# Three attention pairs turned by transposing DMAs instead of TensorE, gate weights prepared on VectorE, four more dummies, and a new order of all engines

## The chip, the cores and the metric

The kernel runs on one core of one Trainium2 chip. The metric is the time of one execution on the device in microseconds, as the median of several runs. Shorter is better. Engines are called as in the profile: PE (TensorE), with PEld for its weight loads, DVE (VectorE), ACT (ScalarE), POOL (GpSimd), and SP, whose queue issues nearly all DMAs.

## The reference

Attention in which a query sees only the keys of its own hash bucket, and after it an RWKV channel mix. Four batches, 8 heads, 768 positions, 64 values a head; the mix has width 512 and 1024 inner units.

```python
q_bits = (einsum('bhsd,dk->bhsk', q, proj) > 0)      # 6 bits a row; k the same
mask = q_bucket[:, :, :, None] == k_bucket[:, :, None, :]
scores = where(mask, scale * (q @ k.T), -1e9)
attn_out = softmax(scores) @ v                       # then x: [4, 768, 512]
x_prev = x shifted by one position
xk = mu_k * x + (1 - mu_k) * x_prev                  # xr the same with mu_r
k = relu(xk @ w_k);  v = (k * k) @ w_v;  r = sigmoid(xr @ w_r)
return r * v
```

## The kernel before

**Work.** Two heads make a pair; there are 16 pairs, four to a batch. Each pair n goes through these steps (the name that the order uses in front):

- `ldq`, `ldv`: loads of q, k and v on SP's queue.
- `hi`, `lo` (L391, L394, DVE): q and k split into a high and a low fp16 half in `nh`; `tr` (L398, SP): a transposing DMA that brings `nh` into `a`, with positions along the free dimension. Pairs 2 and 3 have one for q and one for k, later pairs one for both.
- `bits` (L418, PE): the six hash projections; `bx` (L421, DVE): their signs; `row` (L438, POOL): copied into rows of `a`, so that a score of rows in different buckets comes out low enough to vanish.
- `sc` (L536, PE): nine score steps of 1024 columns; `exp` (L540, ACT): their exponentials into `pt`.
- `vsum` (POOL) and, from pair 4 on, `mean` (PE) and `va`, `mc` (DVE): v with its mean taken off.
- `oo` (L558, L563, PE): the product with v in three groups a head; `rc`, `ob` (DVE): division into `ob`.
- the turn of `ob` into `xt` (model dimension on partitions). Pairs in `OT_PE` use six PE transposes (`ot`, L591) and one DVE copy out of PSUM (`xt`, L594); all others use a transposing DMA on SP's queue (`otd`, L597).
- `xs`, `df`, `xk`, `xr` and their helpers (DVE): the shift and the two mixtures.

Pairs 0 and 1 have no `tr`: PE turns q and k itself (`y`, L473, and `t`, L504), with `x` (L481), a matmul with the gate weights `pw`, giving their bits. `pw` (L702) is the projection with its sign turned, laid out for two heads; it needs the load `pj`.

When the four pairs of batch b have their mixtures, the channel mix follows: `kp` (L651, PE) with `relu` (ACT) and `sq` (DVE), `r` (L671, PE) with `tanh` (ACT), `v` (L684, PE), `os` (DVE), `st` (SP, the store). `wl` and `wc` load the mix's weights and cast them on POOL; `muk` and `mur` load the two mixing vectors, and a small nameless DVE operation each (L270) takes one off.

At the start PE runs matmuls with zeros, called dummies here (`warm`, L247). They compute nothing that is used.

**Order.** `Plan.add` numbers all operations in the order of the program text and notes their dependencies. `ORDER` is a fixed list of these numbers: every engine issues its own operations in this order, and waits where a dependency is not met. `BANKS` gives each PSUM user its place: steps `sc` and `bits` take two of the eight banks, other users one; a user waits until the one before it in its bank has been read. So an operation can wait for its inputs, for its bank, or for what stands ahead of it in its own queue.

```python
    NWARM = 20
    OT_PE = (0, 1, 2, 3, 15)
        if n in OT_PE:
            add("PE", 6 * 0.056, ft, r=["idb", ("ob", so, 0), ("ob", so, 1)], w=[(nm,)], take=("sm", nm, 0), name=nm)
            add("DVE", DVE_C(768, 2), fx, r=[(nm,)], w=[("xt", sx)], give=[nm], name=f"xt{n}")
        else:
            add("SP", 1.25, fd_, r=[("ob", so, 0), ("ob", so, 1)], w=[("xt", sx)], svc=0.95, tr=1, name=f"otd{n}")
```

Of the kernel before, what the change touches and what calls it, by code (L numbers as in the profile page):

```python
# [13 lines left out]
ALU = mybir.AluOpType  # L14
# [114 lines left out]
def kernel(  # L129
# [13 lines left out]
    nc = tc.nc  # L143
# [15 lines left out]
    NWARM = 20  # L159
# [4 lines left out]
    MERGED = tuple(range(4, 16))  # L164
    FIRSTS = (0, 1)
    ROW_SP = ()
    OT_PE = (0, 1, 2, 3, 15)
    QS = 4.0
    ESC = (D ** -0.5) / (QS * QS)
    BITW = 4096.0  # L170
# [594 lines left out]
```

## Time and profile before

| What | Value |
|---|---|
| median of 3 runs | 246.25 us (245.77 to 246.52) |
| profiled execution | 244.73 us |
| its span | 243.0 us |
| PE busy | 234.2 us (96%) |
| DVE busy | 187.6 us (77%) |
| ACT busy | 182.6 us (75%) |
| POOL busy | 95.9 us (39%) |
| granted PE clock | 1.00 |
| DMA queue of SP | 72272 packets, 43.40 MB, 70.7% of 16 engines |

Times inside the kernel are counted from the start of the span. Busy time is that of the engine's own instructions; the share of the DMA engines is a mean over sixteen and reaches a little over 1 where all are busy. The profiled execution is a single one and is shorter than the three timed ones.

### The profile page before, as it was taken

To read this page: it belongs to the slowest core of one execution; us is meant where nothing else is said; L and a number is where in the kernel's file an instruction comes from. 1 tells how busy PE (TensorE), PEld (TensorE's weight loads), DVE (VectorE), ACT (ScalarE), POOL (GpSimd) and SP (SyncE) were. 2 spreads that over 40 slices of the span, in tenths; PEclk is the share of its full clock that TensorE was granted. 3 is DMA by queue.
4 is the path that set the end of the run, shared out by engine and by line. 5 is a ranking of instruction groups with operands and counts; after the bars stand their busy time and mean duration, and the time that the engine had idled before them with its cause. 6 is when DMAs were issued, how large, how long until landed. Compare 5 with 4: busy or idle time off the path is not lost.

```text
span 243.0 us, 6250 instructions
## 1 busy us (share of the span) xinstructions
PE 234.2 (96%) x2522; PEld 147.3 (61%) x2522; DVE 187.6 (77%) x388; ACT 182.6 (75%) x242; POOL 95.9 (39%) x150
## 2 busy tenths in 40 slices
PE   8998999999999899999999999999999999999994
PEld 6975676765567446465556665465566765455443
DVE  3489899999899989699999989936745476966142
ACT  3689999999989689698877998777679871165230
POOL 5465797885919673428036230093500000000000
PEclk9999999999999999999999999999999999999999
DMA  6989999999999999999989683464310403041033
GB/s 229 370 243 197 219 259 230 356 204 348 245 217 233 367 281 208 259 272 264 222 195 233 155 162 85 146 114 126 120 46 0 35 3 119 0 173 47 0 131 132
DMA packets 72526, 44.01 MB, mean 181 GB/s; under 512 B 54832, under 2 KB 67504, under 8 KB 72496
## 3 DMA queue, kind: packets, MB, share of 16 engines
q1 hardware_dynamic: 72272, 43.40, 70.7%
q8 instruction: 20, 0.33, 0.6%
q10 hardware_dynamic: 224, 0.20, 0.2%
q14 instruction: 10, 0.08, 0.1%
HBM read 24.12 MB, written 6.29 MB: 125 GB/s over the span
## 4 chain that ended last, share of the span: by engine, by line
PE 55%; DVE 6%; DMA 3%; issue 1%; DVEq 0%
PE ps_all L684 15%; PE ps_all L651 13%; PE ps_all L536 11%; PE ps_all L671 8%; PE ps_all L563 6%; DMA a<-nh 3%; PE ps_all L418 2%; DVE xk L636 1%; DVE tm L633 1%; DVE nh L391 1%; DVE nh L394 1%; DVE df L622 0%; DVE os L691 0%; DVE va L373 0%; DVE bx L421 0%
## 5 line engine op out<-in xcount | busy, mean ns | idle before, releaser
L540 ACT ACTIVATE pt<-ps_all 128x1024 bf16<-128x1024 f32 x144 | 139.1, 1040 | 19.8 <-PE ps_all L536 18.7
L536 PE MATMUL ps_all<-a 128*128 128x256 f16 (+1 forms) x384 | 79.2, 325 | 2.0 <-ACT pt L540 1.1
L438 POOL COPY a<-bx 6x384 f32<-6x384 f32 x56 | 38.9, 696 | 54.5 <-DVE bx L421 42.3
L563 PEld LDWEIGHTS <-pt 128*128 128x128 bf16 x1152 | 43.7, 97 | 11.6 <-issue 2.1
L651 PE MATMUL ps_all<-xk,wk 128*128 128x384 bf16 x256 | 49.6, 326 | 0.3 <-DVE xk L636 0.3
L536 PEld LDWEIGHTS <-a 128*128 128x128 f16 x384 | 33.7, 98 | 24.9 <-issue 3.5
L684 PE MATMUL ps_all<-wv,k 128*128 128x512 bf16 (+2 forms) x208 | 46.7, 363 | 0.0
L563 PE MATMUL ps_all<-va,pt 128*128 128x65 bf16 x1152 | 46.2, 193 | 0.4 <-DVE va L373 0.4
L658 DVE TENSOR_TENSOR k<-kr 128x384 bf16<-128x384 bf16 x64 | 25.8, 424 | 14.1 <-ACT kr L655 13.8
L655 ACT ACTIVATE kr<-ps_all 128x384 bf16<-128x384 f32 x64 | 29.6, 497 | 7.7 <-PE ps_all L651 6.7
L651 PEld LDWEIGHTS <-wk 128*128 128x128 bf16 x256 | 24.0, 98 | 15.5 <-issue 0.3
L674 ACT ACTIVATE rs<-ps_all 128x512 f32<-128x512 f32 x24 | 14.3, 603 | 23.0 <-DVE os L691 11.7
L684 PEld LDWEIGHTS <-k 128*128 128x128 bf16 x208 | 19.6, 98 | 19.1
L691 DVE SCALAR_TENSOR_TENSOR os<-rs,ps_all 128x512 f32<-128x512 f32 (+2 forms) x26 | 16.7, 643 | 14.9 <-PE ps_all L684 10.8
L394 DVE SCALAR_TENSOR_TENSOR nh<-nat,nh 128x1536 f16<-128x1536 f32 (+1 forms) x16 | 25.7, 1607 | 0.2
L671 PE MATMUL ps_all<-wr,xr 128*128 128x512 bf16 x96 | 24.5, 379 | 0.0
L349 POOL TENSOR_TENSOR vt<-vn 128x384 f32<-128x384 f32 x12 | 14.4, 1200 | 10.8 <-DMA vn<-in_v_dram 7.1
L581 DVE TENSOR_TENSOR ob<-ps_all,rc 128x384 bf16<-128x384 f32 x32 | 17.5, 552 | 0.7
L391 DVE TENSOR_SCALAR nh<-nat 128x1536 f16<-128x1536 f32 (+1 forms) x16 | 15.8, 989 | 1.5 <-DMA nat<-in_k_dram 0.9
L671 PEld LDWEIGHTS <-xr 128*128 128x128 bf16 x96 | 8.7, 97 | 9.5 <-issue 0.6
L421 DVE TENSOR_SCALAR bx<-ps_all 128x768 uint16<-128x768 uint16 x14 | 13.3, 952 | 1.2 <-PE ps_all L418 0.8
L373 DVE SCALAR_TENSOR_TENSOR va<-ps_all,vn 128x384 bf16<-128x384 f32 x24 | 12.8, 549 | 1.4 <-ACT pt L540 0.9
(77 smaller groups left out, 190.6 us busy)
## 6 DMA issues: line engine op xcount, KB each, us to landing
vn<-in_v_dram SPq DMA_DIRECT2D x16, 384.0 KB, 5.1
out_dram<-os SPq DMA_DIRECT2D x23, 256.0 KB, 2.5
nat<-in_q_dram SPq DMA_DIRECT2D x15, 384.0 KB, 4.6
nat<-in_k_dram SPq DMA_DIRECT2D x15, 384.0 KB, 5.3
wst<-in_moe_w_k_dram SPq DMA_DIRECT2D x2, 512.0 KB, 7.2
wst<-in_moe_w_r_dram SPq DMA_DIRECT2D x2, 512.0 KB, 6.2
wst<-in_moe_w_v_dram SPq DMA_DIRECT2D x2, 512.0 KB, 5.9
k<-in_moe_w_k_dram SPq DMA_DIRECT2D x1, 512.0 KB, 7.8
```

The costliest lines, as they stand in the source:

```text
L391: nc.vector.tensor_scalar(out=nh[:, :, 0:D], in0=nat.rearrange("p j (c d) -> p (j c) d", d=D), scalar1=QS, scalar2=None, op0=ALU.mult)
L394: nc.vector.scalar_tensor_tensor(out=nh[:, :, D:P], in0=nat.rearrange("p j (c d) -> p (j c) d", d=D), scalar=QS, in1=nh[:, :, 0:D], op0=AL ...
L438: nc.gpsimd.tensor_copy(side_a[side][sa][D : D + NB, j, :].bitcast(FP32), bx_t[sx][32 * i : 32 * i + NB, :].bitcast(FP32))
L536: nc.tensor.matmul(ps[:, lo - s * STEP : hi - s * STEP], side_a["k"][sa][:, j, jc * P : (jc + 1) * P], side_a["q"][sa][:, j, q0 : q0 + hi ...
L540: nc.scalar.activation(out=pt_t[sp][:, s * STEP : (s + 1) * STEP], in_=ps_t[plan.slot[nm]], func=AF.Exp, bias=EBIAS, scale=ESC)
L563: nc.tensor.matmul(oo[:, ic * 65 : ic * 65 + 65], pt_t[sp][:, o : o + P], va_t[sa][:, j, jc, 0 : D + 1], start=(not uc and ic == 0 and jc ...
L581: nc.vector.tensor_tensor(out=ob_t[so][:, :, j * D : (j + 1) * D], in0=oo[:, :, 0:D], in1=rc_t[sr][:, 1, :].unsqueeze(2).to_broadcast([P, ...
L651: nc.tensor.matmul(ps[:, 0:HALF], wk_sb[:, d, fc * P : (fc + 1) * P], xk_t[mx[d]][:, h * HALF : (h + 1) * HALF], start=(d == 0), stop=(d = ...
L655: nc.scalar.activation(out=kr_t[sk], in_=sm(nm)[:, 0:HALF], func=AF.Relu, scale=0.5 ** 0.5)
L658: nc.vector.tensor_tensor(out=k2_t[s2][:, h * HALF : (h + 1) * HALF], in0=kr_t[sk], in1=kr_t[sk], op=ALU.mult)
L671: nc.tensor.matmul(sm(nr), xr_t[mx[d]][:, c * P : (c + 1) * P], wr_sb[:, d, :], start=(d == 0), stop=(d == NDC - 1))
L684: nc.tensor.matmul(sm(nv)[:, x0:x1], k2_t[(b * NFC + fc) % NK2][:, c * P : (c + 1) * P], wv_sb[:, fc, x0:x1], start=(fc == 0), stop=(fc == ...
```

## The change

1. `OT_PE` loses pairs 0, 1 and 2: their turn goes to transposing DMAs (`otd0` to `otd2`) on SP's queue. Pairs 3 and 15 stay on PE.
2. The two operations that make `pw` move from POOL to DVE.
3. `NWARM` goes from 20 to 24.
4. `ORDER` and `BANKS` are new throughout.

```diff
-    NWARM = 20
+    NWARM = 24
...
-    OT_PE = (0, 1, 2, 3, 15)
+    OT_PE = (3, 15)
...
         for e in range(2):
-            add("POOL", 0.2, lambda e=e: nc.gpsimd.tensor_scalar(out=pw[e * D : (e + 1) * D, e * NB : (e + 1) * NB], in0=pj, scalar1=-1.0, scalar2=None, op0=ALU.mult),
+            add("DVE", 0.1, lambda e=e: nc.vector.tensor_scalar(out=pw[e * D : (e + 1) * D, e * NB : (e + 1) * NB], in0=pj, scalar1=-1.0, scalar2=None, op0=ALU.mult),
```

What the new order moves, by the names above (the lists themselves are only numbers):

- PE, head: 18 dummies stand first in both orders. Then y0q0 before y0k0, and all four `t` of pair 0 ahead of the first score step sc0_3 (before: three). The other six dummies lie among the score steps of pair 0 (before: two).
- PE, up to 58 us: bits2 follows 11 score steps instead of 13; the `oo` groups of pair 0 stand between score steps instead of in blocks of three; sc2_2 precedes bits3; sc3_2 and one `oo2` group precede bits5; sc5_7 precedes bits6.
- PE, later: both matmul groups of kp0_7_1 come after sc7_6; kp1_1_0 stands ahead of r0_5, sc10_4 and two `oo9` groups; the first `kp3` stands ahead of both halves of v2_4_0.
- DVE: bx5 and the second ob2 come ahead of hi6; lo9 follows bx8 at once; xk7 comes ahead of hi12; the operations on muk and mur come among those of pairs 1 and 2; os2_1_0 comes between rc15 and the last ob15.
- SP, up to tr8: ... ldq3k, muk, mur, ldq3q, ldv3, tr2, ldq4q, tr2, ldq4k, ldq5k, tr3, tr3, ldq5q, ldv4, tr4, ldq6q, **otd0**, wl3, **otd1**, tr5, ldq6k, wl2, wl0, **otd2**, wl1, tr6, ldq7k, ldq7q, ldq8q, ldv5, ldq8k, ldv6, wl4, ldv7, tr7, ldq9k, wl5, otd4, ldq9q, wl7, wl6, tr8. Before: ... tr4, ldq6q, tr5, ldq6k, ldv4, wl1, wl0, wl2, wl3, tr6, ldq7q, ldv6, ldq7k, ldq8k, ldv5, wl4, ldq8q, ldq9q, tr7, ldv7, otd4, wl5, tr8, wl8, wl6, wl7, wl9, ldq9k.

120 rows, old and new, of tables (BANKS, ORDER) are left out of this document.

## The prediction

> **What bounds the kernel now.** I read, in this order, the busy time by stage (cut where the exponentials begin, where the first channel-mix matmuls come in, and where TensorE stops pausing), the waits of TensorE, the timelines of ScalarE and TensorE around those waits, and the DMA issues. The columns of the stage view are: the stretch, its length, busy time (and instructions) of PE, PEld, DVE, ACT and POOL, granted clock, DMA share, GB/s.
>
> ```profile
> 12.80:30.00 17.20, 16.17 (x210) 11.29 (x207) 15.20 (x21) 16.44 (x18) 11.55 (x13) 1.00 0.97 213
> 30.00:58.00 28.00, 27.02 (x412) 18.42 (x410) 27.59 (x46) 27.78 (x31) 22.35 (x25) 1.00 1.07 271
> 58.00:80.00 22.00, 21.63 (x294) 14.80 (x291) 20.53 (x41) 19.96 (x29) 15.20 (x20) 1.00 1.08 252
> 80.00:118.00 38.00, 36.18 (x372) 20.77 (x371) 34.28 (x66) 31.54 (x38) 19.94 (x28) 1.00 1.08 271
> 118.00:240.00 122.00, 121.57 (x1146) 71.64 (x1145) 84.59 (x204) 80.52 (x119) 20.36 (x32) 1.00 0.42 105
> ```
>
> There are three regimes. To 58 us ScalarE never rests: from 30 to 58 it is busy 27.78 of 28.00, exponential behind exponential, with VectorE (27.59) and the DMA engines (share 1.07) as full. From 58 to 118 nothing is quite full and TensorE pauses now and then. From 118 on TensorE does not pause. So the end is the moment at which TensorE becomes solid, plus the work then left to it. What may be won lies in pauses, and these are few (waiting engine and line, releaser: us in total, times, longest):
>
> ```profile
> PE ps_all L418 <- DMA a<-nh: 1.3, 2, 0.8
> PE ps_all L247 <- DVE k L244: 1.2, 1, 1.2
> PE ps_all L536 <- ACT pt L540: 1.1, 4, 0.4
> PE ps_all L536 <- DVE ob L581: 0.8, 1, 0.8
> ...
> PE ps_all L651 <- DVE xk L636: 0.3, 1, 0.3
> ```
>
> Two are bits steps (L418) that wait for a transposing DMA of q and k, one is a score step (L536) whose PSUM bank VectorE frees late, one waits for xk. ScalarE's own pauses in the first regime:
>
> ```profile
> 25.33 3.77 ACT L540 ACTIVATE pt<-ps_all 128x1024 bf16<-128x1024 f32 x4 [0.17 <-PE ps_all L536]
> 29.50 1.99 ACT L540 ACTIVATE pt<-ps_all 128x1024 bf16<-128x1024 f32 x2 [0.40 <-PE ps_all L536]
> ```
>
> **Part by part.** The profiled execution took 244.73 us (span 243.0 and 1.7 around it). It is 1.5 below the median 246.25 of the timed runs, and below their lowest, 245.77; I work out a difference against 244.73 and put it on the median.
>
> *Turning pairs 0, 1, 2 by DMA.* Gone from TensorE: 3 x 6 transposes, some 0.34 us a pair by their starts (31.01 to 31.34 for the first), 1.0 in all. Gone from VectorE: three PSUM copies.
>
> ```profile
> L594 DVE COPY xt<-ps_all x5: 543/550/558, 31.5 to 207.3; 128x768 bf16<-128x768 bf16 x5
> ```
>
> That is 3 x 0.55 = 1.65 us. But the 49th exponential, of score step sc5_2, has the same 48 ahead of it on ScalarE in both orders, and ahead of sc5_2 TensorE has the same work but for these 18 transposes and four dummies. Since ScalarE sets the pace there, the freed 1.0 us becomes waiting for a PSUM bank: I count 0 for it. (If TensorE set the pace it would be -1.0; that end is kept.) Added are three transposing DMAs on SP's queue. One alone, at 172.2, and a stretch that holds mostly loads:
>
> ```profile
> 41.00:47.00 6.00, 6.00 (x105) 4.11 (x104) 5.93 (x9) 6.00 (x7) 5.14 (x6) 1.00 1.04 399
> 172.20:175.20 3.00, 3.00 (x16) 1.44 (x15) 2.65 (x7) 1.95 (x3) 2.08 (x4) 1.00 0.33 66
> ```
>
> 0.33 of 3.00 us is 1.0 us of all sixteen engines for 66 GB/s x 3.00 = 198 KB; loads move as much in 0.5 us. So 3.0 us of transfer go into a stretch where the share is 1.07 already. [...]
>
> *Who stands behind them.* The first goes between pair 6's q load and a weight load, the second just ahead of tr5 (the transposing DMA of pair 5's q and k), the third two places ahead of tr6. What such an issue costs SP's queue (tile xt: least, median, longest), and when tr5 and tr6 issue now (SP's timeline: start, us):
>
> ```profile
> L597 SPq DMA_TRANSPOSE xt<-ob x11: 1212/1222/2999, 66.7 to 200.2; - x11
> ...
> 34.12 4.48 SPq L398 DMA_TRANSPOSE a<-nh  x1
> ...
> 47.37 4.21 SPq L398 DMA_TRANSPOSE a<-nh  x1
> ```
>
> The second can issue only when both halves of ob1 are done. Those were ready at 35.64; without xt0 and with bits2 and bits3 placed better I take 35.0, plus 1.22 of issue, so tr5 issues at 36.2 instead of 34.12 and lands about 2.0 later (42.7 for 40.67). bits5 started at 42.88 and now stands behind one more score step and one more PV group (0.43 + 0.36), so that is just covered. Pair 6's k load, behind tr5, lands at 44.6 for 42.6; with bx5 (0.95) and ob2 moved ahead of it, hi6 starts near 45.3 and lo6 ends near 48.0 for 47.23; tr6 lands near 55.7 for 55.02. bits6 waited 0.47 us for tr6 and has one more score step (sc5_7) ahead now, so ScalarE has 0.9 us more to chew on: I charge 0.3, with 0 and +2.1 (all 3.0 us of transfer reach tr6, less 0.9) as ends.
>
> *The new order to 58.* bits2 comes two score steps earlier, and PV groups are spread between score steps; sc2_2 now precedes bits3, which waited for tr3. That takes away the reasons of the two ScalarE pauses, 0.17 + 0.40 = -0.6 (end: 0).
>
> *Head.* The gate weights pw were made on POOL from 5.26 to 6.22, and the first L481 matmul began at 6.28. On VectorE (two of some 0.15 us, by its 128x1 operation of 0.15) they are ready near 5.6, but y0k1 starts at 5.84 for its own load: 0.1 won. One more transposing group (t0q1, 0.33) stands ahead of the first score step: +0.2 (-0.1 to +0.3). Dummies: 18 stand at TensorE's head in both orders. The four new ones, 0.11 each, lie at 13 to 17 us among score steps; there ScalarE runs 0.2 us or more behind TensorE, which hides them; without it they cost 0.4. The minus-one on mur and muk (0.4 and 0.2 us of VectorE at 36 to 37) moves to 13 to 17 and their loads move up past ldq3q, ldv3 and tr2; VectorE stands there until they land, near 14.5, about when the second hi2 began before (14.93): 0 (to +0.5).
>
> *58 to 118.* After sc5_2 the work left to TensorE is equal in both orders. Pauses that go: (a) 0.81 at 97.52, bits9 for tr9. Pair 9's k load moves from behind the last weight loads to just behind tr7, and lo9, which ended at 90.14, has 2.8 us less ahead on VectorE (va7 twice, df4, xra4, sq0_7 twice and small ones): tr9 issues near 87.3 and, at 7.3 to landing, is there at 94.6, before TensorE is (96.7). (b) 0.76 at 82.19: sc7_6 no longer takes the bank of ob6 but that of sc7_0, whose exponential (1.02) fits into the 1.4 us of work between. (c) 0.30 at 118.09: xk7 has 3.2 us less ahead (hi12, xr5, one each of va9, rc8, ob8), its matmul 2.0 us less. Together -1.9. A new order brings tight places of its own; sq0_7, now behind lo9, is one. I put back 0.5: -1.4 (ends -1.9 and +1.0).
>
> *118 to the end.* No pause to lose, only to gain. The first matmuls of the last channel mix (kp3) move ahead of both halves of v2_4 (1.7 us), and xk15, which they need and which was 0.57 early, gets os2_1 (0.69) ahead of it; the last PV group comes 1.7 earlier. I find it 0.2 us early still. sc14_3 moves up 2 us towards its row on POOL. +0.4 (0 to +1.7). The last stores keep their spacing: 0.
>
> Sum: +0.2 - 0.6 + 0.3 - 1.4 + 0.4 = -1.1; 244.73 becomes 243.6, the median **245.1**.
>
> **Rivals.** *The transfers come late (slower).* SP's queue and the DMA engines are full from 28 to 58, and tr5, ldq6k and tr6 stand behind the three additions. If 3.0 us reach tr6, bits6 and the exponentials behind it lose 2.1 us net, and the loads of pair 7, which hi7 awaited at 58.6, pass it on: +2.1 + 0.2 - 0.6 + 0.4 = +2.1 with the gains of 58 to 118 lost, 248.3. It decides once tr6 lands later than about 56.4. For it: the share of 1.07. Against: tr3 and tr4 come sooner, ldv6 leaves the place ahead of pair 7's k load. [...]
>
> *The late stages pause (slower).* xk15 is 0.9 late for the earlier kp3, sc14_3's row 0.8, and the middle gives only -0.7: with +0.2 - 0.3, +0.9, 247.2. Against: the slacks above.
>
> *Nothing moves.* One set of pauses replaces another: 246.25. For: three engines equally full. That the change does not do what it says is possible in one part only, the dummies at the head, which stand as they stood.
>
> **Chances.** Forecast 0.45, nothing 0.17, late transfers 0.22, late pauses 0.16. 0.3% (0.74 us) is about what a measurement tells from no change: faster 0.45, same 0.17, slower 0.38. Range: below, all middle pauses and ScalarE's go and the 1.0 of TensorE counts half (-1.9 - 0.6 - 0.5 = -3.0), 243.2; above, late transfers with a little of the late pauses, 248.6.
>
> **What would show it.** Right: ScalarE without pause from 25 to 31; TensorE without the waits on ob and on tr9; tr6 landing before 56.4; the solid stretch beginning with the same work left, a microsecond sooner. Wrong: bits5, bits6 or hi6 waiting for DMA by over 1 us; TensorE waiting for xk15 near 210 us, or for PSUM banks after 118; or the freed transposes showing up in full, so that TensorE and not ScalarE paced 30 to 58.

## The result: slower, 250.5 us where 245.1 was forecast

| | median | lowest to highest | runs | ratio to before (95%) |
|---|---|---|---|---|
| before | 246.01 us | 244.95 to 246.52 | 4 | |
| changed | 250.53 us | 248.65 to 252.72 | 4 | 1.0151 (1.0104 to 1.0199) |
| changed, timed again (x11 below) | 248.74 us | 247.06 to 252.82 | 9 | 1.0090 (1.0053 to 1.0127) |

The change costs time, and the forecast's range (to 248.6) does not hold the measured 250.53. Medians here and below are over all runs, while the ratios leave out runs more than 1.5% above the fastest of the same kernel (one in the first row for the changed kernel, three in the second). By mean granted TensorE clock, the 13 runs of the changed kernel fall into two groups: 7 have 0.998 to 1.000 and take 247.06 to 249.03 (median 248.65); 6 have 0.986 to 0.993 and take 250.12 to 252.82 (median 251.5). The profiled execution has 0.993 and one slice of 3.41 us at half clock; by that slice length, 0.986 would be two (an estimate: 1.7 us of 248 each). The kernel before ran 92 times beside the experiments, never below 0.997. So there are two things to explain: 2.6 us at full clock, and nearly 3 us more in about half of the runs. The profiled execution (250.12, span 248.3, clock 0.993) has both.

**The profile after.** Busy time by stage, with the columns of the prediction (stretch, length, PE, PEld, DVE, ACT, POOL, clock, DMA share, GB/s):

```profile
12.80:30.00 17.20, 16.47 (x171) 12.23 (x170) 12.93 (x19) 15.15 (x17) 10.30 (x14) 0.95 1.05 237
30.00:58.00 28.00, 26.00 (x403) 17.27 (x402) 24.36 (x38) 27.12 (x31) 21.36 (x26) 1.00 1.08 230
58.00:80.00 22.00, 20.25 (x251) 13.13 (x248) 20.63 (x39) 19.21 (x27) 12.24 (x17) 1.00 1.16 304
80.00:118.00 38.00, 37.28 (x424) 22.28 (x422) 34.69 (x65) 33.09 (x41) 23.21 (x30) 1.00 1.02 228
118.00:240.00 122.00, 121.37 (x1149) 71.04 (x1148) 86.25 (x206) 82.58 (x120) 23.31 (x35) 1.00 0.45 112
```

ScalarE, the pacer to 58 us, is no longer full there (15.15 of 17.20 for 16.44; 27.12 for 27.78), VectorE is emptier still, and the first stretch has a clock of 0.95. TensorE is emptier from 58 to 80 (20.25 for 21.63) and fuller from 80 to 118 (37.28 for 36.18). Its waits (waiting engine and line, releaser: us in total, times, longest):

```profile
PE ps_all L536 <- ACT pt L540: 1.6, 3, 1.0
PE ps_all L418 <- DMA a<-nh: 1.2, 1, 1.2
...
PE ps_all L473 <- DMA nat<-in_k_dram: 0.7, 1, 0.7
PE ps_all L536 <- DVE mc L380: 0.6, 1, 0.6
PE ps_all L684 <- DVE os L691: 0.5, 1, 0.5
```

The wait of a score step on ob (L581) is gone, and so are both that bits6 and bits9 had on transposing DMAs; in their place stand a longer one on the exponentials (1.6 for 1.1), one of 1.2 us on tr5 (bits5, L418), one on the k load in the head, and small ones on mc and os. What the turn costs by tile xt (least, median, longest, first and last start), the issues on SP and the copies left on VectorE:

```profile
L597 SPq DMA_TRANSPOSE xt<-ob x14: 1212/1217/2580, 34.8 to 203.6; - x14
...
L594 DVE COPY xt<-ps_all x2: 549/554/559, 56.7 to 211.8; 128x768 bf16<-128x768 bf16 x2
```

Three copies fewer and three issues more, as the change says. ScalarE's exponentials, timeline (start, length, count, idle before):

```profile
19.13 28.63 ACT L540 ACTIVATE pt<-ps_all 128x1024 bf16<-128x1024 f32 x31 [0.25 <-PE ps_all L536]
48.62 10.32 ACT L540 ACTIVATE pt<-ps_all 128x1024 bf16<-128x1024 f32 x11 [0.86 <-PE ps_all L536]
```

The longest run of exponentials without a pause is 31, from 19.13 on; the forecast was no pause from 25 to 31 us. Then comes one pause that was not forecast, 0.86 us, behind bits5. SP's queue shows why (start, length of issue):

```profile
34.85 2.58 SPq L597 DMA_TRANSPOSE xt<-ob  x1
...
38.15 1.22 SPq L597 DMA_TRANSPOSE xt<-ob  x1
39.47 4.53 SPq L398 DMA_TRANSPOSE a<-nh  x1
...
51.98 4.21 SPq L398 DMA_TRANSPOSE a<-nh  x1
```

The first transposing DMA held the queue for 2.58 us. A weight load and the second one followed (its input ob1 was done at 37.84, just before the queue came to it), and tr5 behind them went out at 39.47 instead of 34.12, although its own input was ready at 36.15. It landed at 47.17 (40.67 before), 7.70 us after its issue where before took 6.55, and bits5 started at 47.21 (42.88).

**Where TensorE loses time.** From the starts of all PE operations I worked out a table. An operation's usual cycle is the median of the shorter half of the distances to the next start, over operations of its kind and size in the kernels compared; what goes beyond it is lost. x7 is the kernel before up to 58 us with the new order behind it (below), x11 the changed kernel again, at full clock.

| stretch, us | before | x7 | changed | x11 |
|---|---|---|---|---|
| 16 to 40 | 3.07 | 3.15 | 1.32 | 1.74 |
| 40 to 58 | 1.37 | 1.36 | 3.34 | 3.59 |
| 58 to 70 | 0.56 | 0.03 | 0.31 | 0.05 |
| 70 to 82 | 0.11 | 2.25 | 2.24 | 2.24 |
| 82 to 100 | 2.01 | 0.73 | 0.62 | 0.71 |
| 100 to 130 | 1.03 | 1.51 | 1.42 | 1.32 |
| 130 to 150 | 0.11 | 1.56 | 1.66 | 1.65 |
| 150 to the end | 0.25 | 0.26 | 0.26 | 0.26 |

The rows are stretches of time, not of work: the first exponential comes at 12.78, 13.15, 16.03 and 13.84 us in the four columns, so the first two rows compare work that is shifted by up to 3 us. Up to 58 us the new order gives back in the second row what it wins in the first. Behind 58 us it loses 6.2 to 6.5 where before loses 4.1, and with before's own first part (x7) it loses the same 6.3. The pauses that the prediction wanted gone are gone (82 to 100); one larger place stands at 70 to 82 (1.0 and 0.6 us in the waits of x7 below), and several small ones stand at 130 to 150, where the longest wait that the view of x7 names is 0.3 us.

The traces can also be cut by work instead of time, at the start of the 49th exponential (sc5_2's). From there to the end of the span it takes 184.0 to 185.3 us in the eight profiles with before's late order (before, x5, x5b, x6, x13, and x10, x16 and x17 with their small moves) and 186.3 to 187.2 in ten with the new one; x1 and x9, which have a half-clock slice in that stretch, take 189. The 49th exponential itself starts at 58.4 to 60.0 with before's first part (before, x7, x10, x13, x16, x17) and, at full clock, at 59.6 to 60.6 with the new one (x4, x8, x11, x12). So at full clock the new late order costs some 2 us, and the new first part about 1.

### The profile page after: what moved, and what is told of

Same layout as the page of the kernel before. It is cut to its first block, busy times and chain, and to the rows that moved or that the text cites. A ratio compares the mean times of both kernels' runs of the same rounds, so it can differ in the third digit from the quotient of the medians.

```text
span 248.3 us, 6224 instructions
## 1 busy us (share of the span) xinstructions
PE 237.4 (96%) x2508; PEld 148.4 (60%) x2508; DVE 188.0 (76%) x387; ACT 183.4 (74%) x242; POOL 95.8 (39%) x148
## 4 chain that ended last, share of the span: by engine, by line
PE 68%; DVE 14%; DMA 7%; ACT 6%; issue 3%; SPq 0%; ACTq 0%
PE ps_all L684 16%; PE ps_all L536 16%; PE ps_all L651 12%; PE ps_all L563 8%; PE ps_all L671 8%; ACT pt L540 6%; DVE k L658 3%; DMA a<-nh 3%; PE ps_all L418 2%; DMA nat<-in_k_dram 2%; PE ps_all L481 2%; DVE nh L391 2%; DMA out_dram<-os 2%; DVE bx L421 2%; DVE nh L394 1%
## 5 line engine op out<-in xcount | busy, mean ns | idle before, releaser
L536 PE MATMUL ps_all<-a 128*128 128x256 f16 (+1 forms) x384 | 80.8, 326 | 3.2 <-ACT pt L540 1.6
L438 POOL COPY a<-bx 6x384 f32<-6x384 f32 x56 | 38.0, 678 | 60.8 <-DVE bx L421 48.7
L563 PEld LDWEIGHTS <-pt 128*128 128x128 bf16 x1152 | 42.8, 97 | 9.2 <-issue 1.2
L684 PE MATMUL ps_all<-wv,k 128*128 128x512 bf16 (+2 forms) x208 | 46.2, 363 | 0.5 <-DVE os L691 0.5
L563 PE MATMUL ps_all<-va,pt 128*128 128x65 bf16 x1152 | 45.1, 193 | 0.0
L655 ACT ACTIVATE kr<-ps_all 128x384 bf16<-128x384 f32 x64 | 30.3, 496 | 18.0 <-PE ps_all L651 10.4
L658 DVE TENSOR_TENSOR k<-kr 128x384 bf16<-128x384 bf16 x64 | 28.1, 455 | 15.1 <-ACT kr L655 14.9
L394 DVE SCALAR_TENSOR_TENSOR nh<-nat,nh 128x1536 f16<-128x1536 f32 (+1 forms) x16 | 26.9, 1679 | 0.2
L349 POOL TENSOR_TENSOR vt<-vn 128x384 f32<-128x384 f32 x12 | 13.7, 1139 | 11.4 <-DMA vn<-in_v_dram 10.8
L581 DVE TENSOR_TENSOR ob<-ps_all,rc 128x384 bf16<-128x384 f32 x32 | 17.6, 553 | 0.6
L391 DVE TENSOR_SCALAR nh<-nat 128x1536 f16<-128x1536 f32 (+1 forms) x16 | 14.8, 922 | 0.1
```

The lines of the kernel that those rows point to most:

```text
L391: nc.vector.tensor_scalar(out=nh[:, :, 0:D], in0=nat.rearrange("p j (c d) -> p (j c) d", d=D), scalar1=QS, scalar2=None, op0=ALU.mult)
L394: nc.vector.scalar_tensor_tensor(out=nh[:, :, D:P], in0=nat.rearrange("p j (c d) -> p (j c) d", d=D), scalar=QS, in1=nh[:, :, 0:D], op0=AL ...
L438: nc.gpsimd.tensor_copy(side_a[side][sa][D : D + NB, j, :].bitcast(FP32), bx_t[sx][32 * i : 32 * i + NB, :].bitcast(FP32))
L536: nc.tensor.matmul(ps[:, lo - s * STEP : hi - s * STEP], side_a["k"][sa][:, j, jc * P : (jc + 1) * P], side_a["q"][sa][:, j, q0 : q0 + hi ...
L563: nc.tensor.matmul(oo[:, ic * 65 : ic * 65 + 65], pt_t[sp][:, o : o + P], va_t[sa][:, j, jc, 0 : D + 1], start=(not uc and ic == 0 and jc ...
L655: nc.scalar.activation(out=kr_t[sk], in_=sm(nm)[:, 0:HALF], func=AF.Relu, scale=0.5 ** 0.5)
```

## The experiments

All ratios are to the kernel before, timed beside the run. Since `ORDER` holds numbers only, edits of the order are shown by operation names.

**1. The late order alone: x7 and x6.**

```diff
 x7:  ORDER of before up to sc5_2 (near 58 us), OT_PE and pw as before
+     then the new ORDER for everything left over
 x6:  new ORDER up to sc5_2 (six dummies as in x4)
+     then the ORDER of before for everything left over
```

> The counterpart: the kernel before (pairs 0 to 2 on TensorE) up to sc5_2, then the changed kernel's order. This is the part of the prediction from 58 us on (-1.4 + 0.4) alone. Prediction's sum: 245.8 - 1.0 = 244.8. New late order pauses more: 245.8 + 2.3 = 248.1. Head and transfers alone: 245.8.

Measured 247.97 for 246.05 of before, ratio 1.0101 (1.0060 to 1.0143). The expectation of the theory that the new late order pauses more was 248.1. TensorE's waits behind 58 us:

```profile
PE ps_all L536 <- ACT pt L540: 1.0, 1, 1.0
PE ps_all L536 <- DVE bx L421: 0.7, 2, 0.4
PE ps_all L536 <- DVE mc L380: 0.6, 1, 0.6
PE ps_all L684 <- DVE os L691: 0.5, 1, 0.5
```

The first and the third are one place, in the changed kernel at 72 us. VectorE's and ScalarE's timelines there, changed kernel:

```profile
70.04 1.25 DVE L627 SCALAR_TENSOR_TENSOR xr<-df,mur,xt 128x768 bf16<-128x768 bf16 x1
71.22 0.65 DVE L658 TENSOR_TENSOR k<-kr 128x384 bf16<-128x384 bf16 x1
```

```profile
71.97 0.87 ACT L655 ACTIVATE kr<-ps_all 128x384 bf16<-128x384 f32 x2 [1.83 <-DVE k L658]
72.72 1.03 ACT L540 ACTIVATE pt<-ps_all 128x1024 bf16<-128x1024 f32 x1
```

xr3 stands ahead of sq0_1 on VectorE; ScalarE's next relu needs the kr buffer that sq0_1 reads and waits 1.83 us; the exponential behind that relu comes late; and TensorE waits for its PSUM bank. xr3 is first used past 82 us, so nothing asked for it there. That this place costs the time is argued from the order of the rows; moving xr3 won nothing (x8 below).

> The changed kernel (six late dummies in the first wait for k, 249.0 as measured) up to score step sc5_2, near 58 us, and the steps left over in the order of before. If the new late order pauses more (by the trace it loses 6.5 us of TensorE behind 58 us where before loses 4.2): 246.5 to 247.3. If all the loss lies in the head and in the late transfers: 248.7 to 249.3. If a pause taken away is given back at the next tight place: about 248.5, with other pauses behind 58 us.

Measured 248.52, ratio 1.0098 (1.0061 to 1.0135), but in two groups: at full clock 246.22, 246.50, 246.61, 247.57 and 248.15, the others at 0.993 from 247.95 up. The first group is what the late order asks for (their mean is some 1.3 under that of the same kernel with the new late order at full clock, 247.64 to 248.98 in x12). bits5 waits 1.8 us for tr5 here, and the half-clock slice follows that wait. So x6 agrees where the clock was full. Its profiled execution (249.60) is one of the others, with the half-clock slice ahead of the 49th exponential, and behind that exponential it takes 185.3 us, as kernels with before's late order do. The full-clock mean, 247.0, is also 1.0 above before's 246.05: that much the new first part costs by itself, with its six late dummies moved. The median alone would also fit the expectation of about 248.5 for a pause given back; the clock is what tells the two apart.

**2. Transposing DMAs in the order of before: x5 and x5b.**

```diff
-    OT_PE = (0, 1, 2, 3, 15)
+    OT_PE = (3, 15)
 SP, x5:   tr4 ldq6q
+          otd0
           tr5 ldq6k
+          otd1
           ldv4 wl1 wl0 wl2 wl3
+          otd2
           tr6
 SP, x5b:  as x5, but otd1 ahead of tr5
 DVE:      xs0 df0 xk0 behind bx4; xs1 df1 xk1 behind lo6; xs2 behind the last ob3
```

> The kernel before with one part of the change alone: pairs 0 to 2 turned by transposing DMAs. On SP the first stands behind pair 6's q load, the second behind tr5 and pair 6's k load, the third just ahead of tr6; on VectorE the shift, difference and xk of pairs 0 to 2 come later, after the transfers have landed. If the transfers themselves cost (3.0 us more for full DMA engines): tr5 or tr6 land 1 us or more later, bits6 starts near 57, time 247 to 248. If only their place in the queue costs: tr6 lands within 0.5 of before (55.0), and the time is 245.0 to 246.3 (between the 1.0 us of TensorE won and nothing). New order: 245.5 to 246.3 too, since the order is that of before.

> As the run with the transposing DMAs in the order of before, but with the second one ahead of tr5 and pair 6's k load on SP's queue, as the changed kernel has it. If the place in the queue costs: tr5 issues near 37 instead of 34, lands near 43.5 and bits5 waits for it by about 0.7 us; the time is 0.5 to 2 more than with the second one behind tr5. If the transfers alone cost, the two kernels agree within 0.5.

Measured 247.85, ratio 1.0067 (1.0039 to 1.0096), for x5, and 250.49, ratio 1.0180 (1.0145 to 1.0214), for x5b: in this order the place of otd1 in SP's queue is worth about 2.6 us. SP's timeline, x5:

```profile
34.03 1.98 SPq L597 DMA_TRANSPOSE xt<-ob  x1
36.12 3.77 SPq L398 DMA_TRANSPOSE a<-nh  x1
```

and x5b:

```profile
34.76 3.05 SPq L597 DMA_TRANSPOSE xt<-ob  x2
37.91 4.32 SPq L398 DMA_TRANSPOSE a<-nh  x1
```

tr5 goes out 1.8 us later, 0.5 of it because all was later by then in this execution (lo5, its input, ended at 34.78 for 34.24). It lands at 44.16 for 42.64, and bits5 starts at 44.20: the wait of 0.7 us that I expected there is not in the trace. Pair 6's k load, behind tr5, lands 3.0 us later, and VectorE stands for it. VectorE's timeline, x5:

```profile
43.87 0.96 DVE L391 TENSOR_SCALAR nh<-nat 128x1536 f16<-128x1536 f32 x1 [0.64 <-DMA nat<-in_k_dram]
```

and x5b:

```profile
46.83 0.96 DVE L391 TENSOR_SCALAR nh<-nat 128x1536 f16<-128x1536 f32 x1 [3.06 <-DMA nat<-in_k_dram]
```

This is hi6, and bx5 stands behind it in before's order, so TensorE waits 1.80 us for bx5 and lo6 ends at 51.01 for 48.06. The changed kernel has bx5 ahead of hi6 and loses 1.2 us at bits5 instead, so the 2.6 us are not what the place costs in its order. x5's own loss is no clean price of the transfers either: its largest wait is 3.6 us of score steps for ob (0.8 before), since the operations that I put behind lo6 hold up ob3 on VectorE. tr6 did land 10.1 us after its issue there (at 58.31; 7.65 and 55.02 before), but bits6, at 58.56, did not wait for it. What the transfers alone cost stays open.

**3. Undoing the transposing DMAs inside the new order: x1, x2, x9.**

```diff
 x1: -    OT_PE = (3, 15)
     +    OT_PE = (0, 1, 2, 3, 15)      # ot0 ahead of sc2_4, ot1 of bits4, ot2 of sc3_1
 x2: SP -  otd1 tr5 ldq6k
        +  tr5 ldq6k otd1
 x9: as x2 and x4, and on DVE xs1 df1 xk1 behind lo6
```

> The changed kernel, but pairs 0 to 2 are turned on TensorE again (six transposes and a PSUM copy each, beside the places where the three transposing DMAs stood); everything else as in the changed kernel. Late transfers: tr5 issues once lo5 is done, near 36.3 instead of 39.5, lands near 43.5 instead of 47.2, bits5 starts near 44.5 instead of 47.2, and the time falls by 1.5 to 3, to 247.5 to 249. Head and clock: the first exponential stays at 16.0, the time stays within 0.7 of 250.5. Later pauses: no change either (250.5), and the distance to before keeps growing behind 58 us.

> The changed kernel with one issue moved on SP's queue: the second transposing DMA (otd1) goes behind tr5 and pair 6's k load instead of ahead of them. All three transfers stay. If the cost is the queue (SP stands at otd1 until ob1 is done, with tr5 behind it): tr5 issues near 36.3, bits5 near 44.5, time 247.5 to 249. If the cost is the DMA engines' time: tr5 still lands near 46 and the time stays near 250. Head and clock: 250.5, no change. Later pauses: 250.5, no change.

> The changed kernel with its six late dummies in the first wait for k (249.0 as measured) and otd1 behind tr5 and pair 6's k load on SP; on VectorE xs1, df1 and xk1, which need otd1, go behind lo6. If tr5's place behind otd1 makes bits5 wait (1.4 us) and hands it on through bx5, hi6, lo6 and tr6: tr5 issues near 36, bits5 starts near 43 instead of 45.5, tr6 lands near 55 instead of 56.7, time 247 to 248. If the DMA engines' time is what is short, tr5 lands later than 44.5 all the same and the time stays at 249.

All three came out slower than the changed kernel: 257.19 (1.0439, 1.0394 to 1.0484), 252.71 (1.0254, 1.0204 to 1.0305) and 253.92 (1.0309, 1.0258 to 1.0359). None answers its question: each has a new and longer wait, and 17 of their 18 runs are below full clock (0.976 to 0.993). In x1 TensorE's largest wait is for the copies that empty the banks of the new transposes:

```profile
PE ps_all L536 <- DVE xt L594: 3.7, 2, 3.0
```

In x2 VectorE, which takes its operations in order, stands at xs1 until the moved otd1 has landed, with ob2 and hi6 behind it:

```profile
48.81 0.20 DVE L604 COPY xt<-xt 128x127 bf16<-128x127 bf16 x1 [3.26 <-DMA xt<-ob]
```

In x9 that is mended, and tr5 still gets out no earlier than 37.22, because the issue of otd0 now takes 3.52 us. In these three, an operation taken out of or moved within an order in which three engines are full cost more than it freed.

**4. The head: x3, x13, x4 and x11 to x15.**

```diff
 x3:  the first 98 steps of before (to its first exponential), pw on POOL, then the new ORDER
 x13: kernel before, pw0 and pw1 on DVE between hi0k0 and hi0k1
 x4:  new ORDER, warm18 to warm23 moved ahead of y0k1
 x11: the changed kernel, unaltered          x12: x4, unaltered
 x14: SP -  ldq0k1 ldq0q1 ldv0 ldq1k
         +  ldq0q1 ldv0 ldq1k ldq0k1
 x15: as x14, NWARM = 48, warm18 to warm47 ahead of y0k1
```

> The order of before up to its first exponential (first 98 steps, the gate weights on POOL again), then the changed kernel's order with what is left. Head and clock: the first exponential starts near 12.8 instead of 16.0, no half-clock window, and the time falls by 2.5 to 3.5, to 247 to 248. Late transfers: the head's gain reaches ob1 and so otd1 and tr5 (37.4 instead of 39.5), but tr5 still stands behind otd1: 248.5 to 249.5. Later pauses: the gain at the first exponential is seen at 58 us and is kept or lost behind it, 248 to 250.

Measured 250.70, ratio 1.0195 (1.0152 to 1.0239). The first exponential came at 13.05, three us sooner than in the changed kernel's profile, and the time did not fall; five of its six runs are at full clock, where the changed kernel takes 248.65, so it is some 2 us slower than that: bits5 waits 1.6 us for tr5, and TensorE 1.1 and 0.6 us for VectorE early on, where the two orders do not fit together. The head's loss was not the whole.

> The kernel before with the gate weights pw prepared on VectorE, between hi0k0 and hi0k1, instead of on POOL; nothing else moves. The prediction gave this 0.1 us, since y0k1 waits for its own load near 5.8: 245.5 to 246.1. Head and clock: if the two operations delay hi0k1 and ey0q0, the first exponential comes 0.3 later and the time is 0.2 more; no half-clock window either way.

Measured 246.70, ratio 1.0032 (1.0008 to 1.0056): no gain, at most a small loss. From y0k1 to the first exponential it is 6.73 us with pw on VectorE and 6.73 with pw on POOL (x7 and x10).

> The changed kernel with its six late dummies moved into TensorE's wait for the k load ahead of y0k1 (5.7 to 7.2 us). Nothing else moves. Head and clock: with TensorE busy through the wait, the half-clock window of 3.41 us at 11.2 does not come, mean granted clock 1.000 in all runs, time 248.3 to 249 (1.7 less than the run with one such window; the head is still some 1.4 late for its loads). If the window has another cause: clock 0.993 as before, time 250 to 250.5. Late transfers and later pauses alone: the time stays at 250.5 whatever the clock.

Measured 248.99, ratio 1.0126 (1.0087 to 1.0166). This looked like the clock's price, but its interval overlaps that of the changed kernel, and the two had not been timed side by side.

> The changed kernel once more, to be timed side by side with the next three. 250 to 250.5; below full mean clock in more than half of its runs, and those runs 1.5 to 2.5 longer than the others.

> The changed kernel with its six late dummies in the wait for k, once more. If the dummies keep the clock: full mean clock in most runs and 1 to 1.7 less than the changed kernel beside it (248.5 to 249.2). If the earlier difference was chance: the same time and the same share of runs below full clock.

Side by side: 248.74, ratio 1.0090 (1.0053 to 1.0127), without the dummies in the wait, and 248.68, ratio 1.0112 (1.0072 to 1.0151), with them; 3 of 9 and 2 of 6 runs below full clock. The 1.5 us of x4 were chance. With the dummies in the wait (x4 and x12) 3 of 12 runs are below full clock, without them 6 of 13: too few to tell apart. What makes the head slow in the changed kernel's profile is the k load for y0k1. It landed at 7.20 there and at 7.71 in x2, but between 5.6 and 6.1 in the other profiles of that head, with the same issues ahead of it. TensorE's clock by stage, changed kernel:

```profile
4.40:7.80 3.40, 2.57 (x22) 2.07 (x20) 0.71 (x3) 0.86 (x2) 0.25 (x1) 1.00 0.97 314
7.80:11.20 3.40, 3.40 (x40) 3.40 (x40) 1.94 (x8) 1.56 (x3) 2.11 (x4) 1.00 1.05 384
11.20:14.60 3.40, 3.40 (x27) 3.40 (x24) 2.67 (x5) 2.28 (x3) 2.16 (x2) 0.50 1.12 321
```

> The changed kernel with the k load that y0k1 needs moved three places back on SP, behind ldq0q1, ldv0 and ldq1k, so that it lands near 9 us in every run and TensorE waits some 2.5 us for it. Clock: a half-clock slice in the head of every run, first exponential near 17.5 to 18, time 251.5 to 252.5. If the slice has nothing to do with the wait: full clock in some runs, 250.5 to 251.5.

> The same late k load, but 30 dummies (the six late ones and 24 more, some 0.11 us each at full clock) between y1q0 and y0k1 keep TensorE at work meanwhile. Clock: full clock in the head, first exponential near 16, and 1 to 1.7 less than with the same late load and no dummies. If the wait is not what sets the clock: the same time as without the dummies, or up to 0.8 more where they outlast the load.

With the load moved back the dummies decide: 258.01, ratio 1.0433 (1.0388 to 1.0478), without them, and 251.47, ratio 1.0207 (1.0175 to 1.0240), with them. The mean granted clock is 0.960 to 0.987 in all six runs of x14, and 0.997 to 1.000 in five of the six of x15 (0.992 in the other). Between 8.0 and 14.6 us, x14:

```profile
8.00:11.20 3.20, 1.62 (x16) 1.62 (x16) 1.25 (x3) 1.03 (x2) 2.65 (x4) 1.00 1.06 390
11.20:14.60 3.40, 3.40 (x26) 3.40 (x26) 0.91 (x4) 0.53 (x2) 1.78 (x3) 0.60 0.99 271
```

and x15:

```profile
8.00:11.20 3.20, 3.20 (x32) 3.04 (x31) 1.33 (x3) 1.09 (x3) 2.40 (x4) 1.00 1.06 391
11.20:14.60 3.40, 3.40 (x45) 3.40 (x45) 1.85 (x6) 1.42 (x4) 2.08 (x3) 1.00 1.09 306
```

In x14's profile TensorE waited 3.1 us for the load, the clock was half from 11.9 to 29.0, five slices in a row, and the first exponential started at 20.99 instead of 16.68. The loss, 6.5 us by the medians and 5.6 by the ratios, is far more than the 1 to 1.7 that I expected of one slice. So a long enough wait in the head, 3.1 us here, cost clock. That the waits of the unaltered changed kernel (0.7 us for this load and 1.2 at bits5 in its profile) are what halves the clock in six of its 13 runs is not shown: only one of those six has a trace.

**5. Is a pause that goes time won? x8, x10, x16, x17.**

```diff
 x8:  x4, DVE -  xr3 sq0_1 va5 mc5 sq0_2
              +  sq0_1 va5 mc5 sq0_2 xr3
 x10: before, SP: ldq9k just behind tr7;  DVE: df4 behind ob6, hi9 ahead of va7
 x16: before, SP: ldq9k just behind tr7;  DVE: hi9 behind mc7, df4 xra4 behind lo9
 x17: x16 and DVE: a va5 ahead of the second sq0_0, xka7 xk7 ahead of hi12
```

> The changed kernel with its six late dummies in the first wait for k (249.0 as measured) and one step moved on VectorE: xr3 (1.25 us, needed only past 80 us) goes behind sq0_1, the second va5, mc5 and sq0_2 instead of ahead of them. If VectorE's order there makes the pause (sq0_1 late, so relu0_3 and with it the exponential of sc6_6 late, so TensorE waits 1.85 us for a PSUM bank ahead of sc6_8): sc6_8's pause falls below 0.7 and the time to 247.5 to 248. Late transfers or head alone: the microsecond is given back at the next exponentials and the time stays at 249.

Measured 248.99, ratio 1.0149 (1.0102 to 1.0197), for 248.99 and 1.0126 (1.0087 to 1.0166) of x4: nothing won. The pause ahead of sc6_8 shrank as expected, and a new one followed 5 us behind it. VectorE is busy for 7.93 of the 8 us from 68 to 76 in this profile and in that of the changed kernel, so a later xr3 makes something else late. TensorE's timeline, x8:

```profile
71.65 0.59 PE L536 MATMUL ps_all<-a 128*128 128x256 f16 x3 [0.51 <-ACT pt L540]
...
76.51 0.59 PE L536 MATMUL ps_all<-a 128*128 128x512 f16 x2 [1.52 <-DVE bx L421]
```

> The kernel before with two moves that the prediction counted as gains (a) and (b), made alone: pair 9's k load on SP just behind tr7 with hi9 on VectorE ahead of va7 (for the 0.8 us of bits9), and df4 (1.39 us) behind ob6 (for the 0.8 us of sc7_6). If a pause that goes is time won: 244.2 to 244.8. If it is given back at the next tight place, as the pause ahead of sc6_8 was: 245.5 to 246.1.

> The kernel before with the two moves of x10 placed so that mc7 is not pushed back: pair 9's k load just behind tr7, hi9 behind mc7, df4 and xra4 behind lo9. If a pause that goes is time won where nothing new is made late: the waits ahead of sc7_6 and sc7_4 are gone, bits9's is half as long, 1.0 to 1.5 less than before (244.6 to 245.1). If it is always given back: no change (245.6 to 246.4).

> The same, with two more moves on VectorE: one va5 ahead of the second sq0_0 (PV group oo5_1 waited 0.5 for it), and xka7 and xk7 ahead of hi12 (kp1_1_0 waited for xk7, 0.5). Time won: 1.6 to 2.4 less than before (243.7 to 244.5). Given back: no change, or tr12 late by the 1.0 us that hi12 moves back.

x10: 245.81, ratio 0.9995 (0.9966 to 1.0024). By the measure of the table above, the pause ahead of sc7_6 went from 0.93 to 0.38 and that of bits9 to nothing, and sc7_4, whose bank waited for the mc7 that I had pushed back, lost 1.22. x16, without that push: 245.87, ratio 0.9984 (0.9956 to 1.0012); in its trace TensorE loses 3.7 us behind 58 us for 4.1 before. Both times are in the range expected if the time is given back. x17: 245.77, ratio 0.9970 (0.9941 to 0.9999), the lowest ratio of all kernels here, about 0.7 us and barely beyond what can be told from no change; 243.7 to 244.5 was expected. Four pauses of 2.9 us by the trace of before bring a quarter of that.

## Why the prediction was wrong

The forecast was 1.1 us faster. Three things went the other way: the new order behind 58 us costs some 2 us where it was to win 1.0, the part up to 58 us costs about 1 where it was to win 0.1, and about half of the runs lose nearly 3 us more to the clock, for which the sum had no term.

**58 us to the end (-1.4 + 0.4): the step that failed.** The gains were real: sc7_6's pause and bits9's wait for tr9 went, and of 2.0 us lost from 82 to 100 only 0.7 are left in x7. tr9 went out at 91.64 instead of the 87.3 that I expected, since the whole kernel was later by 4, and still landed before TensorE was there. What failed is the term "I put back 0.5" for the tight places of the new order. It measured about 3.5: 2.14 more than before at 70 to 82, 0.48 at 100 to 130, 1.45 at 130 to 150, less 0.53 at 58 to 70. So -1.0 became +2.3 by the trace, and x7 measured +1.9 by the medians and +2.5 by its ratio (+1.5 to +3.5). That is most of the 2.6 us at full clock, but not all: x6 puts about 1.0 on the first part. The gains were over-counted too: in before's own order, four pauses of 2.9 us brought 0.7 (x17), so a pause removed is not time won in full. I had gone through the waits of before one by one and asked whether each survives, but compared the new order with the old only around those places. xr3 ahead of sq0_1 could be read off the order: kr has four buffers, and the exponentials stand behind the relus. It is an example of such a place; moving it alone won nothing (x8). That the new late order costs them is shown (x7, x6); which of its places would have to change stays open.

**tr5 and tr6 (+0.3).** The expectation for tr5 (issue 36.2, landing 42.7) was missed by 3.3 and 4.5 us. Three terms were wrong: the issue of a transposing DMA in a full queue took 2.58 us where I took the median 1.22 (the row that I quoted had 2.999 as its longest); ob1 was done at 37.84 instead of 35.0, with a late head; and tr5 took 7.70 us from issue to landing where I kept 6.5 (7.6 to 8.6 in x3, x4, x6, x8, x11 and x12, which have the same order there; 5.47 in x1, where the two additions ahead of it are gone). With an early head, in x11, tr5 went out at 37.01, only 0.8 late, but landed 8.19 us later, at 45.20, and bits5 waits 1.4 us. The cover that I named, two more operations ahead of bits5, was too thin. x5b against x5 shows that the queue place can cost, though there by the way of pair 6's k load and not of bits5. tr6's +0.3 came out as nothing: bits6 did not wait for it.

**ScalarE's pauses (-0.6).** Right: no pause between 19 and 47 us, and TensorE loses 1.3 to 1.8 us less from 16 to 40, as far as that row compares the same work. The 2.0 to 2.2 us lost behind bits5 ate it up.

**The head (+0.2).** Two parts. With an early load the first exponential comes at 13.72 (x1) and 13.84 (x11), against 13.05 to 13.15 in the profiles with before's head and full clock from 5.0 to 5.2 on (x3, x5, x7; 5.6 and 5.3 in x1 and x11): +0.6 or 0.7. A part of that is the later clock and not the order: in x10, with before's head and full clock from 6.7 on, the first exponential comes at 13.87. The rest, the half-clock slice, I had not thought of: I wrote that the dummies "stand as they stood" and asked only whether they delay other work, not whether TensorE's waits, here and behind bits5, are long enough to halve the clock. pw: 0.1 won was wrong by its sign if anything (x13).

**The rivals.** "Late stages pause" had the right stretch, a smaller size (247.2; measured 248.65 at full clock) and none of the right places: xk15 and sc14_3 cost nothing (0.26 us lost behind 150 us, 0.25 before). "The transfers come late" was right about tr5 and not about what it named as decisive: tr6 landed at 58.01 in the profile, past 56.4, and bits6 did not wait for it. That its 248.3 is close to 248.65 is luck.

## What to carry to other kernels

Where three engines are full, the price of a new order is in its new tight places: read each engine's new queue for a long operation that stands ahead of a short one for which another engine waits, with buffer counts in hand, before counting any pause as won. A transposing DMA put ahead of others costs the queue the wait for its own input as well as its issue (in the changed kernel's profile the queue was free at 46.50, otd2 went out at 48.01, when ob2 was done, and its issue took another 1.22). Time the early and the late half of a new order by themselves before explaining single waits. And ask of every wait of TensorE whether it is long enough to cost clock as well (3.1 us in the head of x14 were; in x6 a half-clock slice followed 1.8 us at bits5).

## What the runs showed of the hardware

In these traces the granted clock changes in slices of 3.41 us: in the changed kernel's trace the half-clock stretch from 11.23 us on is 3.413 us long, and the full-clock stretches ahead of it and behind it are 6.827 and 235.520 us, 2 and 69 times as long. In the middle of the kernel the profiles have seven half-clock slices, in x1, x2, x5, x5b, x6 and x9, each behind a slice in which TensorE was busy for 9 to 46% of the time; stage view of x5, two slices:

```profile
49.50:52.90 3.40, 1.32 (x20) 0.92 (x19) 3.33 (x6) 1.88 (x3) 2.82 (x4) 1.00 1.22 174
52.90:56.30 3.40, 3.40 (x43) 2.74 (x41) 2.32 (x7) 3.03 (x4) 3.21 (x5) 0.50 1.65 254
```

TensorE was busy for 1.32 of 3.40 us, and the next slice ran at 0.50; x1 has the same with 1.17, x6 with 1.57 of 3.41. One slice that was 44% busy, in x1, kept the clock, so these cases do not show where the limit lies. In the head of the changed kernel the half clock came one slice later, after 2.57 of 3.40, a slice with full busy time between; why, the runs do not tell, nor why x14 had five half-clock slices in a row (mean clock 0.967 over 257.8 us).

The issue of the same kind of transposing DMA of ob took SP's queue between 1.2 and 3.5 us. Even otd0, in one place of the same order, took 1.22 in x6, 1.64 in x11 and 2.58 in the changed kernel's profile; what decides it, the runs do not tell. The k load for y0k1, third on SP's queue in both orders, landed anywhere from 5.6 to 7.7 us after the start from one execution to the next. And the clock first became full at a moment between 3.9 us (before) and 7.2 us (x13), at 4.4 and 5.3 us in two executions of the changed kernel (its profile and x11); in before the dummies follow each other by 0.21 us up to that moment and by 0.11 us behind it. Where it was late, as in x13, the first 15 fp32 transposes of the head took 2.88 us instead of 1.90 (before).
